# The inverse of the softmax sums on VectorE in place of ScalarE, with a new order of the work

## The chip, the cores and the metric

The kernel runs on one core of a Trainium2 chip. The metric is the device time of one execution in microseconds (us). Every comparison is between runs on the same chip. The profile names the engines PE (TensorE matmuls), PEld (TensorE weight loads), DVE (VectorE), ACT (ScalarE), POOL (GpSimd) and SP (SyncE, which issues most DMAs).

## The reference

The program is a transformer block over 2048 tokens of width 640: layernorm, an attention with a recurrent memory and a residual, then layernorm, a gated feed-forward part (width 1728) and a residual. The attention goes through 64 segments of 32 tokens in sequence. Each segment attends to 8 memory rows and its own 32 tokens, with 32 heads of 128, and the memory of the next segment is the attention's output at the 8 memory rows. So segment s + 1 cannot start its projections of the memory before segment s is through its output projection.

```
mem = mem0
for s in range(n_seg):
    h = jnp.concatenate([mem, xs], axis=1)          # 8 + 32 rows
    q, k, v = h Wq, h Wk, h Wv                      # per head
    scores = where(mask, q k^T * scale, -1e9)
    p = _softmax(scores, axis=-1)
    o = (p v) Wo
    mem = o[:, :M, :]
    outs.append(o[:, M:, :])
```

The softmax divides the exponentials by their sum over the 40 keys. The kernel computes the inverse of each sum and multiplies the exponentials by it. That inverse is what the change is about.

## The kernel before, in words

Weights are loaded once and stay in SBUF. The attention's main part treats 32 rows per segment, the 8 memory rows and the first 24 tokens; the last 8 tokens of the segments do not depend on the memory, and their projections are made ahead, 32 rows at a time for four segments, by `rest` (from L1567), as work that fills gaps of the recurrence. Layernorms (`ln1`, `ln2`), and the output projection of the 8 last tokens (`rest_o`, L1637), are such fill work too. After the 64 segments comes the feed-forward part (`ffn`, L1717).

One segment (`segment`, L1839) does the following, in two groups g of 16 heads:

- `main_qk` and `main_v` project the 32 rows to queries, keys and values (L1561 is the matmul of all projections). The results are evacuated from PSUM to `tok` (Q0ev, K0ev, Q1ev, K1ev) and turned by VectorE's 32x32 transposes into QT and KT (Q0Tev, K0Tev, Q1Tev, K1Tev, L1981), or evacuated to `Vm` (V0ev, V1ev). Evacuations go through the helper at L1399 to L1402: L1401 is the ScalarE form, L1402 the VectorE form.
- `scores(g)` (L1851): the mask is written into a PSUM bank (seed), TensorE adds the scores to it (sc, L1860 and L1864), ScalarE takes the exponentials into E (exp, L1869), and TensorE sums them over the keys by matmuls with a block of ones (sum, L1874 and L1539), into columns 224 to 384 of the same bank, so that each sum stands at the partitions of its keys, 128x160 in fp32.
- The inverse of the sums is made by ScalarE in two instructions: the logarithm of the bank into `lnS` (L1882), then exp(-x) of `lnS` into `rS`, in bf16 (L1884). VectorE multiplies E by rS in place (mul, L1886). There is one lnS and one rS for both groups, so the second group's inverse waits until the first multiplication has read rS.
- `pv(g)` (L1892): TensorE multiplies the scaled exponentials with the values (L1899 and L1904), and two copies bring the result to `oT` (oTev).
- The output projection: group 0 by `wo_early` (L1932), whose result is split into two bf16 halves (hiev, loev at L1940), group 1 by `wo` (L1951), to which the halves are added by matmuls (woadd, L1968; L1539 again). `mem_next` (L1665) copies the memory rows into the next input (L1673) and transposes it to xT (L1676), which the next segment's projections read.

**The order of the work** is set by a list scheduler in the kernel's own code (`_Sched`). Every step is declared with its engine or engines, its reads and writes, and a duration `dur`. Its level is the longest path of declared durations from it to the end, plus two numbers from the table BIAS: one for its name ("rec0": the inverse of group 0) and one for its name in one segment ("rec0@20"). Among steps that can start at nearly the same time on an engine the one with the highest level goes first. Each engine then has one fixed order of instructions, with semaphore waits on the others. For evacuations that ScalarE or VectorE could do, the table ENGINE fixes the engine, by name or by name and segment; those that are not in it go where the declared durations let them end first. BIAS and ENGINE hold numbers found by a search. DMAs are issued in the same way, mostly on SP's queue.

Of the kernel before, what the change touches and what calls it, by code (L numbers as in the profile page):

```python
# [6 lines left out]
F32 = mybir.dt.float32  # L7
# [15 lines left out]
BIAS = {"ldrs": 7992.0, "ldv": 8028.08, "QK0mm": 104.65, "r0Tev": 14.09, "memev": 167.3, "ln2n": 144.44,  # L23
# [12 lines left out]
    "ordma": 158.72, "oTr": 169.2, "rsdma": -179.29, "l1e2": 169.29, "down": -59.94, "ln2Tev": -117.41,  # L36
# [7 lines left out]
    "K0T": 89.89, "QK1mm": 50.37, "free": -27.64, "ervdma": -169.96, "erdma": -49.67, "rvdma": 188.66,  # L44
    "free0": -32.62, "woadd": -36.1, "sel2": 60.17, "loev": -192.29, "hiev": 1.72, "ezero": 80.29,
# [1216 lines left out]
def build_kernel(nc, A_x, A_mem0, A_Wq, A_Wk, A_Wv, A_Wo, A_seg_len, B_x, B_W_gate, B_W_up,  # L1262
# [108 lines left out]
    def bank(b):  # L1371
        return ps[:, b.at * 512:(b.at + 1) * 512]
# [774 lines left out]
```

## Time and profile before

Three runs took 1050.64, 1051.72 and 1053.94 us. The rest of the table is from one profiled execution.

| what | value |
| --- | --- |
| median of the runs | 1051.72 us |
| span of the profiled execution, first to last instruction | 1051.2 us |
| mean granted TensorE clock | 0.995 |
| TensorE busy | 993.4 us, 95% |
| VectorE busy | 652.5 us, 62% |
| ScalarE busy | 488.1 us, 46% |
| logarithm of the sums (L1882, ScalarE) | 128 x 302 ns |
| exponential of its negative (L1884, ScalarE) | 128 x 336 ns |
| multiplication of E by the inverse (L1886, VectorE) | 128 x 334 ns |
| first, middle and last stage of the span | 0 to 75, 75 to 862, 862 to 1051.2 us |

How to read it: in the first stage the weights come in and the first segments run, in the middle stage run nearly all segments, the last stage is the feed-forward part. The profile gives for each group of instructions its busy time, the mean duration of one, and the idle time of the engine just before it with what ended that idle time. Matmuls are pipelined, so that a busy TensorE is not yet one at its peak. A weight load that waits is the first sign that TensorE's queue waits. For the profiled execution there is the span and no other time; it lies 0.5 us under the median of the runs.

### The profile page before, as it was taken

How to read it: one execution, taken by the hardware profiler on the slowest of the kernel's cores; microseconds unless marked ns; L12 is line 12 of the kernel's file. 1: busy time of each engine (PE TensorE's matmuls, PEld its weight loads, DVE VectorE, ACT ScalarE, POOL GpSimd, SP SyncE). 2: the span in 40 equal slices, each digit the busy share in tenths (PEclk: the TensorE clock that was granted, in tenths of full speed). 3: DMA queues.
4: the chain of work that ended last, by engine and by line, in shares of the span. 5: the costliest groups of instructions: out<-in, count | busy, mean ns of one | idle time of the engine just before them, and what ended most of it. 6: DMA issues, size and time to landing. Idle time of an engine off the chain costs nothing.

```text
span 1051.2 us, 53190 instructions
## 1 busy us (share of the span) xinstructions
PE 993.4 (95%) x24820; PEld 534.8 (51%) x23828; DVE 652.5 (62%) x1404; ACT 488.1 (46%) x1161; POOL 108.4 (10%) x262
## 2 busy tenths in 40 slices
PE   5699999999999999999999999999999989999998
PEld 2245555655565555655555555655555444444443
DVE  4457767677777767776777677667865642432233
ACT  2334555455556545555665455645554632121210
POOL 2301101011011101110101011011110010000000
PEclk9999999999999999999999999999999999999999
DMA  9991112121222112221222122212211237111101
GB/s 328 397 286 47 49 37 55 32 54 50 80 54 73 38 42 60 73 66 33 80 69 54 32 69 58 66 28 76 70 49 31 77 117 219 65 38 44 32 20 57
DMA packets 119212, 84.26 MB, mean 80 GB/s; under 512 B 71556, under 2 KB 115148, under 8 KB 118988
## 3 DMA queue, kind: packets, MB, share of 16 engines
q1 hardware_dynamic: 115628, 78.13, 24.9%
q8 instruction: 191, 3.13, 1.3%
q10 hardware_dynamic: 3360, 2.73, 0.8%
q14 instruction: 33, 0.27, 0.1%
HBM read 55.05 MB, written 25.69 MB: 77 GB/s over the span
## 4 chain that ended last, share of the span: by engine, by line
PE 86%; DVE 4%; ACT 2%; issue 2%; DMA 1%; ACTq 0%; POOL 0%; SPq 0%
PE ps L1561 45%; PE ps L1729 11%; PE ps L1932 7%; PE ps L1951 7%; PE ps L1762 5%; PE ps L1647 3%; PE ps L1899 2%; PE ps L1539 2%; PE ps L1874 1%; PE ps L1860 1%; DVE xT L1676 1%; DVE xm L1673 1%; DVE oT L1402 1%; DMA RS<-stg 1%; ACTq L1605 0%
## 5 line engine op out<-in xcount | busy, mean ns | idle before, releaser
L1401 ACT ACTIVATE tok<-ps 128x512 bf16<-128x512 f32 x241 | 142.2, 596 | 177.6 <-PE ps L1561 162.5
L1561 PE MATMUL ps<-Wk,xT 128*32 128x512 bf16 x2560 | 178.0, 380 | 14.2 <-DVE xT L1676 10.2
L1561 PE MATMUL ps<-Wq,xT 128*32 128x512 bf16 x2560 | 178.4, 379 | 6.1 <-DVE xT L1676 6.0
L1561 PE MATMUL ps<-Wv,xT 128*32 128x512 bf16 x2560 | 175.2, 380 | 0.2 <-DMA Wv<-in_A_Wv_dram 0.2
L1981 DVE STREAM_TRANSPOSE KT<-tok 128x512 bf16<-128x512 bf16 x128 | 89.6, 704 | 35.2 <-ACT tok L1401 33.7
L1981 DVE STREAM_TRANSPOSE QT<-tok 128x512 bf16<-128x512 bf16 x128 | 90.3, 706 | 32.8 <-ACT tok L1401 30.1
L1561 PEld LDWEIGHTS ps<-Wk,xT 128*32 128x32 bf16 x2560 | 67.1, 96 | 82.3 <-DVE xT L1676 20.9
L1561 PEld LDWEIGHTS ps<-Wq,xT 128*32 128x32 bf16 x2560 | 67.5, 96 | 72.2 <-DVE xT L1676 12.2
L1402 DVE CAST oT<-ps 128x320 bf16<-128x320 f32 x127 | 60.3, 488 | 54.7 <-PE ps L1904 51.8
L1932 PE MATMUL ps<-Wo,oT 128*32 128x320 bf16 x2048 | 90.9, 300 | 3.3 <-DVE oT L1402 3.2
L1951 PE MATMUL ps<-Wo,oT 128*32 128x160 bf16 x4096 | 86.2, 233 | 6.6 <-issue 4.9
L1746 ACT ACTIVATE g<-ps 128x512 bf16<-128x512 f32 (+1 forms) x56 | 33.4, 596 | 124.8 <-PE ps L1729 124.8
L1951 PEld LDWEIGHTS ps<-Wo,oT 128*32 128x32 bf16 x4096 | 74.3, 97 | 22.2 <-DVE oT L1402 9.5
L1748 DVE TENSOR_TENSOR gT<-g,ps 128x512 bf16<-128x512 bf16 (+1 forms) x56 | 37.5, 686 | 77.3 <-PE ps L1729 47.1
L1401 ACT ACTIVATE oT<-ps 128x320 bf16<-128x320 f32 x129 | 54.0, 435 | 54.9 <-PE ps L1904 53.2
L1561 PEld LDWEIGHTS ps<-Wv,xT 128*32 128x32 bf16 x2560 | 59.7, 96 | 38.0 <-ACT tok L1401 1.0
L1846 POOL COPY QT<-RS 128x256 bf16<-128x256 bf16 x64 | 25.8, 403 | 457.6 <-PE ps L1864 457.1
L1402 DVE CAST tok<-ps 128x512 bf16<-128x512 f32 x79 | 52.9, 670 | 24.8 <-PE ps L1561 24.5
L1869 ACT ACTIVATE E<-ps 128x224 bf16<-128x224 f32 x128 | 45.6, 356 | 43.0 <-PE ps L1864 42.2
L1729 PE MATMUL ps<-xn2T,Wg 128*128 128x512 bf16 x260 | 63.3, 379 | 0.3 <-DVE gT L1748 0.3
L1729 PE MATMUL ps<-xn2T,Wu 128*128 128x512 bf16 x260 | 63.3, 379 | 0.0
L1762 PE MATMUL ps<-Wd,gT 128*128 128x512 bf16 x224 | 61.7, 379 | 0.0
(93 smaller groups left out, 1444.6 us busy)
## 6 DMA issues: line engine op xcount, KB each, us to landing
RS<-scr_qk SPq DMA_DIRECT2D x63, 128.0 KB, 2.3
big<-in_A_x_dram SPq DMA_DIRECT2D x36, 160.0 KB, 2.8
scr_qk<-stg SPq DMA_DIRECT2D x44, 128.0 KB, 2.2
Wq<-in_A_Wq_dram SPq DMA_DIRECT2D x10, 512.0 KB, 7.3
Wk<-in_A_Wk_dram SPq DMA_DIRECT2D x10, 512.0 KB, 7.4
Wv<-in_A_Wv_dram SPq DMA_DIRECT2D x10, 512.0 KB, 8.1
Wo<-in_A_Wo_dram SPq DMA_DIRECT2D x8, 640.0 KB, 10.8
scr_v<-stg SPq DMA_DIRECT2D x32, 128.0 KB, 2.7
```

The costliest lines, as they stand in the source:

```text
L1401: return e.activation(dst, src, ACTF.Copy)
L1402: return e.tensor_copy(dst, src)
L1561: o = pe.matmul(out, lhs[c], rhs, start=(c == 0), stop=(c == DC - 1), skip_group_check=True)
L1647: o = pe.matmul(bank(bk)[p0:p0 + 32, 0:2 * SLICE], oTr[b][:, 16 * g + 4 * j + i, 32 * y:32 * y + 32], cols(h, 2 * a, 2 * a + 2), start=(h ...
L1729: o = pe.matmul(bank(bk)[:, 0:TB], lhs(c), xT[:, :, c * 128:(c + 1) * 128], start=(c == 0), stop=(c == DC - 1))
L1746: op("act", lambda a, t=t, lo=lo, hi=hi, bg=bg: a.activation(g1[t.at][lo:128, :], bank(bg)[0:hi, 0:TB], ACTF.Relu), r=["B2"], x=[bg, t], d ...
L1748: op("dve", lambda v, t=t, lo=lo, j=j, bu=bu: v.tensor_tensor(gT[lo:128, j, :], g1[t.at][lo:128, :], bank(bu)[lo:128, 0:TB], ALU.mult), r= ...
L1762: pe.matmul(bank(ba)[:, 0:512], lhs, Wd[:, j, 0:512], start=(j == 0), stop=(j == FC - 1), skip_group_check=True)
L1869: op("act", lambda a: a.activation(E[:, g, :, 0:56], sco(BS[g]), ACTF.Exp, scale=SCALE), r=["table"], w=[("E", g)], x=[BS[g]], dur=0.36, n ...
L1932: o = pe.matmul(bank(BA)[p0:p0 + 32, 0:2 * SLICE], oT[:, 4 * jj + i, XR:40], cols(h, 2 * b2, 2 * b2 + 2), start=(i == 0 and jj < 2), stop= ...
L1951: o = pe.matmul(bank(BW)[32 * j:32 * j + 32, 0:SLICE], oT[:, 16 + 4 * jj + i, XR:40], cols(h, j, j + 1), start=(i == 0 and jj == 0), stop= ...
L1981: op("dve", lambda v, tb=tb, dst=dst: v.transpose(dst, tok[tb.at][:, :].rearrange("p (h r) -> p h r", r=32)), w=[("QT" if p == 0 else "KT" ...
```

## The change

The inverse of the sums is one VectorE instruction, a reciprocal that reads the sums in PSUM and writes rS in bf16. The logarithm and the exponential of ScalarE go away, and with them the tile lnS. The step keeps its name (rec0, rec1) and its declared duration of 0.33. Nothing else of the computation changes.

All numbers of BIAS and ENGINE are others: BIAS goes from 3499 entries to 3410 with none of them equal, ENGINE from 689 to 442. So the order of the instructions on every engine, and the engine of many evacuations, change too. Of those that the tables fix on VectorE over the 64 segments: V0ev from 23 to 3, V1ev from 44 to 1, K0ev from 24 to 1, K1ev from 5 to 3, Q0ev from 8 to 10, Q1ev from 33 to 48. Before, 30 of Q0ev and 24 of K1ev were left to the declared durations; after, none of these six names.

```
-BIAS = {"ldrs": 7992.0, "ldv": 8028.08, "QK0mm": 104.65, "r0Tev": 14.09, "memev": 167.3, "ln2n": 144.44,
...
-    "er1T": 151.28, "er0T": 20.42, "ln1T": 213.1, "sum1": 44.27, "rec0": -93.01, "ln2nd": 109.66,
...
-    "mul0": 111.45, "mask0": 49.23, "Q1Tev": 309.11, "ln0": 40.86, "mask1": 16.89, "V1mm": -24.65,
...
+    "Q1ev": 317.41, "Q1Tev": 643.59, "K1ev": -113.73, "K1Tev": -250.28, "V1mm": -33.96, "V1ev": -82.6,
+    "seed0": -24.36, "sc0": -20.28, "exp0": -610.44, "sum0": 35.39, "rec0": -70.29, "mul0": 375.41,
...
-    "K0ev": "dve", "er0ev": "act", "r1ev": "dve", "rvev": "act", "Q0Tev": "act", "osbev": "act",
...
+ENGINE = {"er0Tev": "act", "er1ev": "act", "Q0ev": "act", "Q0Tev": "act", "K0ev": "act", "K0Tev": "act",
+    "V0ev": "act", "Q1ev": "dve", "Q1Tev": "dve", "K1ev": "act", "K1Tev": "act", "V1ev": "act", "seed1": "act",
...
@@ -1323,7 +1270,6 @@
     E = ar.alloc("E", [128, 2, 4, 80], BF16)
-    lnS = ar.alloc("lnS", [128, 160], F32)
     rS = ar.alloc("rS", [128, 160], BF16)
...
@@ -1879,10 +1825,10 @@
-            op("act", lambda a: a.activation(lnS[:, :], bank(BS[g])[:, 224:384], ACTF.Ln),
-               r=["table"], w=["lnS"], x=[BS[g]], dur=0.3, name=f"ln{g}")
-            op("act", lambda a: a.activation(rS[:, :], lnS[:, :], ACTF.Exp, scale=-1.0),
-               r=["lnS"], w=["rS"], dur=0.33, name=f"rec{g}")
+            def inverse(v):
+                with nc.allow_low_precision(reason="the sums' inverses are of the inputs' type"):
+                    return v.reciprocal(rS[:, :], bank(BS[g])[:, 224:384])
+            op("dve", inverse, w=["rS"], x=[BS[g]], dur=0.33, name=f"rec{g}")
```

More of the change, by code (lines that the diff above doesn't have):

```diff
@@ L22 @@
 ADD = 4
-BIAS = {"ldrs": 7992.0, "ldv": 8028.08, "QK0mm": 104.65, "r0Tev": 14.09, "memev": 167.3, "ln2n": 144.44,
[12 rows of a table removed]
-    "ordma": 158.72, "oTr": 169.2, "rsdma": -179.29, "l1e2": 169.29, "down": -59.94, "ln2Tev": -117.41,
[7 rows of a table removed]
-    "K0T": 89.89, "QK1mm": 50.37, "free": -27.64, "ervdma": -169.96, "erdma": -49.67, "rvdma": 188.66,
-    "free0": -32.62, "woadd": -36.1, "sel2": 60.17, "loev": -192.29, "hiev": 1.72, "ezero": 80.29,
[586 rows of a table removed]
-ENGINE = {"Q1Tev": "dve", "r0Tev": "act", "V1ev": "dve", "l1e0": "dve", "l1e2": "dve", "ln2Tev": "act",
-    "K0ev": "dve", "er0ev": "act", "r1ev": "dve", "rvev": "act", "Q0Tev": "act", "osbev": "act",
[131 rows of a table removed]
+BIAS = {"sel2": -441.65, "ezero": 172.26, "ldxrs0": 410.57, "ldxrs1": 812.23, "ldxra": -143.87, "ldxrl": 370.82,
+    "ldxrx": -190.47, "ldxrn": -453.78, "ln1rT": -359.59, "l1r": -21.49, "ldxs0": 455.91, "ldxs1": -311.66,
+    "ldxa": 459.65, "ldxl": 162.16, "ldxx": -63.35, "ldxn": 474.64, "ldxx0": -54.04, "ldxst": 103.86,
+    "ldxxm": -394.13, "ldmev": 106.07, "ones": 26.56, "mem": 217.62, "mem1": 70.53, "er0mm": -202.35,
[19 rows of a table added]
+    "tn2nd": 179.14, "gu": -56.84, "relu": 128.7, "gmul": -267.28, "hld": 284.67, "down": -60.53,
[583 rows of a table added]
+ENGINE = {"er0Tev": "act", "er1ev": "act", "Q0ev": "act", "Q0Tev": "act", "K0ev": "act", "K0Tev": "act",
+    "V0ev": "act", "Q1ev": "dve", "Q1Tev": "dve", "K1ev": "act", "K1Tev": "act", "V1ev": "act", "seed1": "act",
+    "r0ev": "act", "r0Tev": "act", "r1ev": "act", "osrev": "act", "ln2Tev": "act", "tn2Tev": "act",
[79 rows of a table added]
 class _Slot:
```

1413 rows, old and new, of tables (BIAS, ENGINE) are left out of this document.

## The prediction

> **What bounds the kernel.** I read the page from the top, then the busy time by stage, then the waits of TensorE's weight loads in the middle stage, and last one segment on VectorE and ScalarE in order of time.
>
> ```profile
> span 1051.2 us, 53190 instructions
> ...
> PE 993.4 (95%) x24820; PEld 534.8 (51%) x23828; DVE 652.5 (62%) x1404; ACT 488.1 (46%) x1161; POOL 108.4 (10%) x262
> ...
> PE 86%; DVE 4%; ACT 2%; issue 2%; DMA 1%; ACTq 0%; POOL 0%; SPq 0%
> ```
> TensorE is busy for 95% of the span and makes up 86% of the chain that ended last; ScalarE, which the change relieves, is 2% of that chain.
>
> ```profile
> core 0: us, PE busy (x) PEld busy (x) DVE busy (x) ACT busy (x) POOL busy (x), PEclk, DMA share, GB/s
> 0.00:75.00 75.00, 52.59 (x988) 22.51 (x980) 34.95 (x80) 21.90 (x46) 18.80 (x47) 0.95 0.98 344
> 75.00:862.00 787.00, 755.76 (x22662) 433.56 (x21902) 560.32 (x1226) 430.15 (x1052) 89.60 (x215) 1.00 0.22 58
> ```
> The middle stage holds nearly all segments. TensorE is idle there for 787.0 - 755.8 = 31.2 us. VectorE is busy for 71%, ScalarE for 55%: the inverse goes from the less busy of the two to the busier one.
>
> ```profile
> PEld ps L1561 <- DVE xT L1676: 32.3, 54, 1.1
> PEld ps L1874 <- ACT E L1869: 26.5, 84, 0.7
> PEld ps L1899 <- DVE E L1886: 20.5, 67, 0.8
> ```
> These are weight loads of the middle stage. The third line is what the inverse can delay: the load of the value product (L1899) waits for the scaled E of L1886 in 67 of 128 groups, 0.31 us each. TensorE itself often still works off earlier matmuls then, so not all of the 20.5 us is lost. I counted the chain that ended last piece by piece: the logarithm (L1882) is on it 10 times with 2.9 us, the exponential (L1884) 10 times with 3.4 us. In the other 118 groups the pair is beside TensorE's work.
>
> **The rows of the change.**
>
> ```profile
> L1882 ACT ACTIVATE lnS<-ps 128x160 f32<-128x160 f32 x128 | 38.7, 302 | 23.7 <-PE ps L1539 23.4
> L1884 ACT ACTIVATE rS<-lnS 128x160 bf16<-128x160 f32 x128 | 43.0, 336 | 4.2 <-DVE E L1886 0.3
> L1886 DVE TENSOR_TENSOR E<-E,rS 128x320 bf16<-128x320 bf16 x128 | 42.8, 334 | 14.8 <-ACT rS L1884 12.2
> L1402 DVE CAST Vm<-ps 128x512 bf16<-128x512 f32 x67 | 45.3, 675 | 4.4 <-PE ps L1561 4.1
> L1402 DVE CAST osb<-ps 128x160 bf16<-128x160 f32 x20 | 5.7, 287 | 9.0 <-PE ps L1539 9.0
> ```
> Removed: 128 x (302 + 336) ns = 81.7 us of ScalarE, of which 6.3 us are on the chain. VectorE's multiplication waited for this pair in only 19 groups (12.2 us, by the waits on rS); in the other 109 VectorE was still busy with something else when the inverse was ready.
>
> Added: 128 reciprocals on VectorE, 128x160, fp32 in PSUM to bf16 in SBUF. No row shows one. The lower bound is the copy of the same shape, between the same memories, on the same engine: 287 ns. The upper bound I build from the slope of the two copy rows, (675 - 287) / (512 - 160) = 1.10 ns per column, so one pass over 160 columns is 0.18 us and 0.11 us is fixed. A quotient has to be developed to the 8 significant bits of the bf16 result; at one pass per bit, that is 0.11 + 8 x 0.18 = 1.5 us, an estimate. For the low end speaks ScalarE, where the logarithm of 160 columns (302 ns) costs what a copy of 160 does. For the high end speaks that every VectorE row of this trace adds, multiplies, compares or moves, so that the copy is near in shape and not in kind, and that the only inverse of the page takes two whole instructions on its engine. I take the upper end, with little lead, and keep both for the range.
>
> [...]
>
> Moved: the tables fix 67 evacuations of V on VectorE in the old order and 4 in the new one. 63 x 675 ns = 42.5 us leave VectorE, and about 63 x 0.59 = 37 us come to ScalarE (its row for V, 591 ns). With the copy's price the reciprocals add 128 x 0.287 = 36.7 us, and VectorE stays where it was; with 1.5 us they add 192 us, and its load in the middle stage is 560 + 189 - 42 = 707 of 787 us, 90%. ScalarE ends lower either way (430 - 80 + 37) and costs nothing. Dropping lnS moves no work. No DMA is added; loads and stores change places only as the new order has it, and the middle stage uses 22% of the DMA engines.
>
> The added wait: the reciprocal waits on VectorE for TensorE's sums. Behind it stand the multiplication, the second query transpose, which the second scores wait for, and the copies of oT, which the output projection waits for. One segment shows what it meets:
>
> ```profile
> 451.81 0.65 DVE L1402 CAST tok<-ps 128x512 bf16<-128x512 f32 x1
> 452.50 0.71 DVE L1981 STREAM_TRANSPOSE QT<-tok 128x512 bf16<-128x512 bf16 x1
> 453.14 0.28 DVE L1886 TENSOR_TENSOR E<-E,rS 128x320 bf16<-128x320 bf16 x1
> 454.23 0.49 DVE L1402 CAST oT<-ps 128x320 bf16<-128x320 f32 x1 [0.81 <-PE ps L1904]
> 454.75 0.69 DVE L1402 CAST Vm<-ps 128x512 bf16<-128x512 f32 x1
> 455.35 0.32 DVE L1886 TENSOR_TENSOR E<-E,rS 128x320 bf16<-128x320 bf16 x1
> 456.25 0.49 DVE L1402 CAST oT<-ps 128x320 bf16<-128x320 f32 x1 [0.59 <-PE ps L1904]
> ```
> Here the first logarithm began at 452.09, while VectorE ran the copy and the transpose of the second queries until 453.21. Put behind that transpose (the new table gives Q1Tev a far higher bias than rec0), a reciprocal of 1.5 us ends at 454.7, the multiplication at 455.0, and the first value product starts 1.2 us late. The second reciprocal runs from 455.0, the second multiplication ends near 456.9 where it ended at 455.67: again 1.2 us. That is one delay, carried along. Put ahead of the transpose, it delays the second scores by 1.5 us and the second value product by about 2.2 us. TensorE's order is fixed, and from the second value product on the segment has no work to spare: output projection, new memory (L1673), its transpose (L1676), next segment. The plan itself is laid for a short reciprocal (the code declares 0.33), so it does not cover the rest.
>
> **The sum.** 63 segments in the stage after the first, times 1.2 us, is 75.6 us. Its own bounds: 0.7 us where VectorE's idle time and fill work on TensorE take part of it (44 us), 1.8 us where the reciprocal often stands ahead of the transpose (113 us). 1051.2 + 75.6 = 1126.8. The median of the runs, 1051.72, is 0.5 us above the profiled span, so I add 0.5: **about 1127 us**, with 1096 to 1165 for this case.
>
> **The rivals.** A difference under 0.3% (3.2 us) is about what a measurement of this kernel cannot tell from none.
>
> Second: the reciprocal costs what the copy costs, and the pair was hidden anyway. The chain gains 6.3 us and pays ten reciprocals, 2.9 us; the new order gives and takes as much. That is 1049 to 1055, say 1051. For it speaks that the pair is on the chain in 10 of 128 groups; against it, that the whole order is another one.
>
> Third, on the other side: at the copy's price the change is faster. The inverse is one instruction of 0.29 us with one handover less, in place of 0.64; the chain gains 6.3 - 2.9 = 3.4 us, and the order, with V's evacuations off VectorE ahead of the transposes, wins back a sixth of TensorE's 31.2 us of idle time, 5.2 us: 1051.7 - 8.6 = 1043, down to 1035 at twice that. It decides from the point where VectorE is free when the sums land. Against it: it was free in 19 of 128 groups.
>
> Fourth: the copy's price, but VectorE is not free. In the 67 groups where the weight load waited for E, 0.287 us is added, 19.2 us, less the 6.3 us that leave the chain: 1051.7 + 12.9 = 1065, and 1055 to 1075.
>
> **How the numbers follow.** Forecast 0.52, second 0.14, third 0.24, fourth 0.10. Slower is first and fourth, 0.62; same 0.14; faster 0.24. The range reaches from 1040, which leaves out about 0.1 of the third rival, to 1165, which leaves out under 0.1 of the forecast; both prices of the reciprocal are in it.
>
> **What would show it.** The reciprocal's row: over 1 us for the forecast, about 0.29 us for the rivals; between them the sum shrinks in proportion. With the forecast, VectorE's busy time in the middle stage rises by over 100 us, the weight loads of L1899 wait for E in nearly all groups and for far more than 20.5 us, and the time comes in the middle stage alone, with the last stage still near 189 us. The forecast is wrong if the row is long and the middle stage is not: then VectorE's idle time (227 us of 787) covered it. If the row is short, second to fourth are told apart by the waits on E and by how often VectorE is busy when the sums land.

## The result and the profile after

The changed kernel takes 1108.96 us, the median of four runs (1106.79 to 1111.61), against 1052.83 us before. The ratio is 1.0538, with a 95% interval from 1.0506 to 1.0570. The profiled execution of the changed kernel has a span of 1109.8 us, 58.6 us more than before.

The page of the changed kernel, its head, busy times and the chain that ended last:

```profile
span 1109.8 us, 53145 instructions
...
PE 995.1 (90%) x24808; PEld 538.0 (48%) x23828; DVE 740.7 (67%) x1432; ACT 465.6 (42%) x1005; POOL 108.2 (10%) x262
...
PE 64%; DVE 24%; ACT 3%; issue 2%; ACTq 1%; DMA 0%; POOL 0%; DVEq 0%
PE ps L1507 30%; DVE rS L1830 13%; PE ps L1675 11%; PE ps L1897 7%; PE ps L1878 4%; PE ps L1708 4%; DVE KT L1927 3%; DVE E L1832 3%; ACT tok L1347 3%; PE ps L1845 3%; DVE oT L1348 2%; PE ps L1485 2%; PE ps L1593 2%; DVE stat L1421 1%; DVE QT L1927 1%
```
TensorE has nearly the same work, 995.1 us after 993.4, now 90% of the span. On the chain VectorE goes from 4% to 24%, and one line of it, the reciprocal (L1830), has 13%. Counted piece by piece, the reciprocal is on the chain 127 times out of 128, with 141 us. The ScalarE pair before was on it 10 times, with 6.3 us.

The rows of the step by form, changed kernel (busy us, mean ns of one, idle time ahead of it and what ended that):

```profile
L1830 DVE RECIPROCAL rS<-ps 128x160 bf16<-128x160 f32 x128 | 147.5, 1152 | 13.0 <-PE ps L1485 12.8
L1832 DVE TENSOR_TENSOR E<-E,rS 128x320 bf16<-128x320 bf16 x128 | 41.5, 324 | 4.1
L1348 DVE CAST Vm<-ps 128x512 bf16<-128x512 f32 x4 | 2.7, 680 | 0.0
```
One reciprocal takes 1.152 us, 3.6 times what the copy of the same shape takes (0.320 us in e1 below). The V evacuations left VectorE as the tables say. And VectorE was idle until the sums came in only 24 of 128 groups; otherwise it was busy when they landed.

The middle stage of the changed kernel, with the columns of before, and who waits there (in the last three fences first the wait of TensorE's matmuls before the change, then the waits of the matmuls and of the weight loads after it; us in all, times, longest):

```profile
75.00:920.00 845.00, 760.07 (x22654) 436.31 (x21891) 647.89 (x1262) 407.91 (x896) 88.36 (x214) 0.99 0.20 53
```
```profile
PE ps L1899 <- DVE E L1886: 0.5, 2, 0.3
```
```profile
PE ps L1845 <- DVE E L1832: 60.3, 98, 1.6
PE ps L1507 <- DVE xT L1622: 5.2, 12, 0.6
```
```profile
PEld ps L1845 <- DVE E L1832: 101.2, 98, 1.8
```
The stage is 58.0 us longer (845.0 against 787.0), nearly all of the 58.6 us, and TensorE is idle in it for 845.0 - 760.1 = 84.9 us, where it was 31.2. The ends of the stage were set by hand, but the feed-forward's own start says the same: its first matmul is at 928.0 us in place of 868.7. The value product's weight loads (L1845; in the kernel before, L1899) wait for the scaled E in 98 groups for 101.2 us, where it was 67 groups and 20.5 us; and now TensorE itself stands still there, 60.3 us, where it was 0.5.

One segment on the chain that ended last (start us, us, what):

```profile
472.35 0.71 DVE KT L1927
473.06 1.12 DVE rS L1830
474.18 0.02 issue
474.20 0.34 DVE E L1832
474.54 0.05 issue
474.58 0.27 PE ps L1845 x16
474.86 0.09 PE ps L1850 x4
474.94 0.02 issue
474.97 0.49 DVE oT L1348
475.46 1.07 DVE rS L1830
476.53 0.03 issue
476.56 0.33 DVE E L1832
476.89 0.05 issue
476.94 0.27 PE ps L1845 x16
```
Every link is VectorE or the value product that waits for it. The first reciprocal begins when VectorE is through a key transpose, the sums having landed just before. The second begins behind the copy of the first product's result (L1348), so it cannot start before the first reciprocal, the first multiplication and the first product are through. In the same segment TensorE stands idle for 0.62 us ahead of the first value product and for 0.64 us ahead of the second. Its rows (the number in brackets is the idle time and what ended it) show a second reason why the second reciprocal is late:

```profile
474.58 0.27 PE L1845 MATMUL ps<-E,Vm 32*128 32x40 bf16 x16 [0.62 <-DVE E L1832]
...
474.82 0.25 PE L1820 MATMUL ps<-E,bones 128*32 128x160 bf16 x4
...
476.94 0.27 PE L1845 MATMUL ps<-E,Vm 32*128 32x40 bf16 x16 [0.64 <-DVE E L1832]
```
TensorE makes the sums of the second group (L1820) only after the first value product, so they too are late when that product is. In this order that is so in 57 of the 64 segments, and in 39 a copy of the first product's result is the VectorE instruction just ahead of the second reciprocal.

### The profile page after: what moved, and what is told of

Same layout as the page of the kernel before. It is cut to its first block, busy times and chain, and to the rows that moved or that the text cites. A ratio compares the mean times of both kernels' runs of the same rounds, so it can differ in the third digit from the quotient of the medians.

```text
span 1109.8 us, 53145 instructions
## 1 busy us (share of the span) xinstructions
PE 995.1 (90%) x24808; PEld 538.0 (48%) x23828; DVE 740.7 (67%) x1432; ACT 465.6 (42%) x1005; POOL 108.2 (10%) x262
## 4 chain that ended last, share of the span: by engine, by line
PE 64%; DVE 24%; ACT 3%; issue 2%; ACTq 1%; DMA 0%; POOL 0%; DVEq 0%
PE ps L1507 30%; DVE rS L1830 13%; PE ps L1675 11%; PE ps L1897 7%; PE ps L1878 4%; PE ps L1708 4%; DVE KT L1927 3%; DVE E L1832 3%; ACT tok L1347 3%; PE ps L1845 3%; DVE oT L1348 2%; PE ps L1485 2%; PE ps L1593 2%; DVE stat L1421 1%; DVE QT L1927 1%
## 5 line engine op out<-in xcount | busy, mean ns | idle before, releaser
L1347 ACT ACTIVATE tok<-ps 128x512 bf16<-128x512 f32 x248 | 147.2, 597 | 220.3 <-PE ps L1507 207.9
L1507 PE MATMUL ps<-Wq,xT 128*32 128x512 bf16 x2560 | 170.6, 379 | 5.4 <-DVE xT L1622 5.2
L1507 PE MATMUL ps<-Wk,xT 128*32 128x512 bf16 x2560 | 171.1, 379 | 4.3 <-DMA Wk<-in_A_Wk_dram 4.2
L1830 DVE RECIPROCAL rS<-ps 128x160 bf16<-128x160 f32 x128 | 147.5, 1152 | 13.0 <-PE ps L1485 12.8
L1347 ACT ACTIVATE oT<-ps 128x320 bf16<-128x320 f32 x144 | 60.8, 436 | 127.9 <-PE ps L1850 126.1
L1507 PEld LDWEIGHTS ps<-Wq,xT 128*32 128x32 bf16 x2560 | 67.2, 96 | 74.6 <-DVE xT L1622 18.3
L1845 PE MATMUL ps<-E,Vm 32*128 32x40 bf16 x2048 | 35.2, 178 | 70.8 <-DVE E L1832 60.7
L1347 ACT ACTIVATE Vm<-ps 128x512 bf16<-128x512 f32 x124 | 74.0, 597 | 29.5 <-PE ps L1507 29.4
L1845 PEld LDWEIGHTS ps<-E,Vm 32*128 32x128 bf16 x2048 | 22.1, 91 | 122.2 <-DVE E L1832 102.0
L1348 DVE CAST oT<-ps 128x320 bf16<-128x320 f32 x112 | 54.1, 487 | 33.0 <-PE ps L1850 32.3
L1347 ACT ACTIVATE ps<-seed 128x384 f32<-128x384 bf16 x109 | 50.2, 487 | 49.6 <-DVE half L1886 42.0
```

Source lines behind the costliest of these rows:

```text
L1347: return e.activation(dst, src, ACTF.Copy)
L1348: return e.tensor_copy(dst, src)
L1507: o = pe.matmul(out, lhs[c], rhs, start=(c == 0), stop=(c == DC - 1), skip_group_check=True)
L1830: return v.reciprocal(rS[:, :], bank(BS[g])[:, 224:384])
L1845: o = pe.matmul(bank(BP[j])[:, 40 * i:40 * i + 40], Vm[32 * j:32 * j + 32, g, i * 128:(i + 1) * 128], E[32 * j:32 * j + 32, g, i, 0:40], s ...
```

## The experiments

Theory A: the length of the reciprocal is the whole loss. The rivals: B, it is the move to VectorE's busy queue or the new order, whatever the instruction costs; C, it is that the plan was laid for 0.33 us and did not know the length. Theories D and E, on how the two groups' delays add up, come with e7 and e8. "New tables" and "the order of the change" are the change's BIAS and ENGINE, "old tables" those of before. The scheduler lays the order from tables and declared durations, so a kernel that keeps both keeps the order, whatever the instruction in the step really is. The runs were made on several chips, each with the kernel before beside it, so times of different runs are compared by their ratios to it; a ratio is turned into us with 1052 us.

### e1: a copy in the place of the reciprocal

```
-                    return v.reciprocal(rS[:, :], bank(BS[g])[:, 224:384])
+                    return v.tensor_copy(rS[:, :], bank(BS[g])[:, 224:384])
```


> The changed kernel with the reciprocal replaced by a copy of the same 128x160 from PSUM to rS, on the same engine, at the same place of the same order; the multiplication then uses the sums themselves, so the scaling is not the reference's. Theory A (the 1152 ns of the reciprocal are the whole loss): the row falls to about 0.29 us, the waits of the value product's weight loads for E fall from 101 us to under 30 us, and the time is 1042 to 1056 us. Rival B (the loss is the move of the inverse to VectorE's queue, or the new order, whatever the instruction takes): 1080 us or more.

1041.81 us; ratio to the kernel before 0.9913 (0.9886 to 0.9940). The step's row, and the waits for E of the value product's weight loads and matmuls:

```profile
L1830 DVE CAST rS<-ps 128x160 bf16<-128x160 f32 x128 | 40.9, 320 | 12.5 <-PE ps L1485 12.0
```
```profile
PEld ps L1845 <- DVE E L1832: 34.8, 92, 1.0
...
PE ps L1845 <- DVE E L1832: 0.8, 1, 0.8
```
Same engine, same place, same order, 0.83 us less in each group: 67 us less (66 by the ratios), just under the range expected, and faster than the kernel before by 0.9%. So the move to VectorE and the new order, taken together, are no loss at the length of a copy; B falls. The weight loads still wait 34.8 us, a little over the 30 expected, but TensorE's own wait for E falls from 60.7 us to 0.8 us: at this length the waiting is covered by matmuls under way.

### e2: the ScalarE pair back, with the new tables

```
-            op("dve", inverse, w=["rS"], x=[BS[g]], dur=0.33, name=f"rec{g}")
+            op("act", lambda a: a.activation(lnS[:, :], bank(BS[g])[:, 224:384], ACTF.Ln), ...
+            op("act", lambda a: a.activation(rS[:, :], lnS[:, :], ACTF.Exp, scale=-1.0), ...
```


> The changed kernel with its new tables, and the logarithm and exponential of ScalarE put back in place of the reciprocal. Theory A: the tables alone cost little, 1045 to 1065 us. Rival B (the new order is what is slow): 1080 us or more.

1092.88 us, ratio 1.0394 (1.0374 to 1.0414). By its expectation this is B, but e1 ran the order of the change at 0.9913, so that order is not slow. e2 does not run it: with other steps the same tables lay another plan (in order of time at most 574 of the change's 1432 VectorE instructions keep their order). That the pair is slow here because the tables were found for another step fits this, and is not shown apart. VectorE now waits for rS (last column: idle ahead of the multiplication):

```profile
L1833 DVE TENSOR_TENSOR E<-E,rS 128x320 bf16<-128x320 bf16 x128 | 41.6, 325 | 64.2 <-ACT rS L1831 63.7
```
64 us of waiting for ScalarE, where it was 12.2 us in all before. Taken alone, this run would have misled.

### e3: only the reciprocal, with the old tables

The kernel before with the hunk on the inverse alone, BIAS and ENGINE as they were.

> The kernel before with its old tables, and only the inverse changed to the reciprocal. Theory A: as slow as the change or slower, since VectorE keeps the evacuations of V too: 1108 to 1135 us. Rival B (the new order is what is slow): clearly faster than the change, under 1090 us.

1159.72 us, ratio 1.1019 (1.0999 to 1.1038): slower than expected, and 50 us slower than the change. The new tables do not make the change slow, they save about half of what this hunk alone costs (10.2% against 5.4%).

### e4: the real length declared, with the new tables

```
-            op("dve", inverse, w=["rS"], x=[BS[g]], dur=0.33, name=f"rec{g}")
+            op("dve", inverse, w=["rS"], x=[BS[g]], dur=1.15, name=f"rec{g}")
```


> The changed kernel with the same tables, and the reciprocal declared to the scheduler at 1.15 in place of 0.33, so that the order is laid for its real length. Theory A (the length is on the recurrence and cannot be filled): 1095 to 1115 us. Rival C (the loss is that the plan did not know the length, and TensorE has fill work to put there): under 1085 us.

1119.71 us, ratio 1.0643 (1.0618 to 1.0667): 11 us slower than the change, above what was expected. Declaring the length is no help without tables found for it. The plan is a different one (at most 671 of 1432 VectorE instructions keep their order): TensorE's wait for E falls from 60.7 to 18.3 us, and its wait for the next segment's input rises from 5.2 to 29.0.

```profile
PE ps L1507 <- DVE xT L1622: 29.0, 56, 1.0
PE ps L1845 <- DVE E L1832: 18.3, 28, 1.6
```
These waits do not explain the 11 us. Over the whole span TensorE is idle for 1118.1 - 1006.6 = 111.5 us, where the change has 1109.8 - 995.1 = 114.7. What is longer is its busy time, by 11.5 us, at a granted clock of 0.985 against 0.993; why, no run shows.

### e5: a copy with the old tables

The kernel of e3 with the copy of e1.

> The kernel before with its old tables, the inverse replaced by a copy on VectorE (so the scaling is not the reference's). With e3 it gives the price of the reciprocal's length in another order; with the kernel before, the price of tables that were searched for another step. Theory A with the length priced as in the new order (1109 - 1042 = 67 us): 1160 - 67 = 1093, so 1080 to 1105 us. Rival B' (in the old tables the reciprocal costs little by its length, and the move to VectorE costs most): 1125 us or more.

1079.79 us, ratio 1.0256 (1.0217 to 1.0296), a hair under the lower edge of what was expected. In the old tables too the length of the reciprocal is what costs: from e5 to e3 (1.0256 to 1.1019) it is 7.6%, 80 us, where it is 66 us in the new ones. (Of the 77.7 us between the two profiled spans, TensorE's idle time makes up 66.7 and its busy time 11.0.) The other 2.6% are what the move to VectorE costs in tables that were found for the pair; no run parts the move from the tables.

### e6: a touch on the plan

The kernel before, the same instructions, the logarithm declared at 0.31 in place of 0.30.

> The kernel before, same instructions and same tables; only the declared duration of the logarithm goes from 0.30 to 0.31, so that the order is laid again without a search. If the tables fit one set of declared durations and no other, the time rises to 1070 to 1100 us, and e2, e3 and e4 each carry such a surcharge. If they are robust: 1050 to 1058 us, and e2's 1093 is a loss of the new order itself.

1055.49 us, ratio 1.0042 (1.0020 to 1.0063). That lies in the range for robust tables, but it tests little, because the plan hardly changed: in order of time up to 1397 of VectorE's 1404 instructions and 1156 of ScalarE's 1161 stand as before. What a plan laid anew costs, as in e2 and e4, this run does not tell, so the surcharges of e2, e4 and e5 stay mixtures of the step and its plan.

### e7 and e8: the reciprocal in one group only

```
-                    return v.reciprocal(rS[:, :], bank(BS[g])[:, 224:384])
+                    f = v.reciprocal if g == 0 else v.tensor_copy      # e8: g == 1
+                    return f(rS[:, :], bank(BS[g])[:, 224:384])
```


> The order of the change, reciprocal in group 0, copy in group 1 (so group 1's scaling is not the reference's). Theory D (the prediction: one delay is carried along, and the second inverse decides): 1042 to 1060 us. Theory E (two separate stalls of TensorE at the two value products, 0.6 us each by the trace): half of the 67 us, 1068 to 1085 us.

> The order of the change, copy in group 0 (so group 0's scaling is not the reference's), reciprocal in group 1. Theory D: nearly all of the 67 us, 1092 to 1110 us. Theory E: about half, 1068 to 1085 us, and the two surcharges of e7 and e8 add up to that of the change.

e7: 1076.63 us, ratio 1.0230 (1.0193 to 1.0268). e8: 1066.65 us, ratio 1.0139 (1.0103 to 1.0175), a little under its range for theory E. Above the copy in both groups (0.9913) these are 3.2% and 2.3%, 33 us and 24 us; together 57 us, where both reciprocals cost 6.25%, 66 us. The waits of TensorE for E, first of e7, then of e8:

```profile
PE ps L1846 <- DVE E L1833: 33.7, 52, 1.6
```
```profile
PE ps L1846 <- DVE E L1833: 27.4, 47, 0.8
```
33.7 us of standing still for 33 us of time, 27.4 us for 24 us. In the traces, e7's wait lies in group 0 alone, e8's in group 1 but for 0.8 us, and the change itself has 33.6 us in group 0 and 27.0 in group 1. There are two stalls in a segment, and they add up to 57 of the 66 us; the other 9 us come only with both reciprocals, and no run says from where. Theory D, one delay that is carried along and decided by the second inverse, falls.

### e9 and e10: other lengths of the step

e9 makes the reciprocal twice, the first time into a scratch tile. e10 makes 80 columns by a copy and 80 by a reciprocal.

```
+                    v.reciprocal(twice[:, :], bank(BS[g])[:, 224:384])                      # e9
                     return v.reciprocal(rS[:, :], bank(BS[g])[:, 224:384])
```
```
+                    v.tensor_copy(rS[:, 0:80], bank(BS[g])[:, 224:304])                     # e10
+                    return v.reciprocal(rS[:, 80:160], bank(BS[g])[:, 304:384])
```


> The order of the change, with the reciprocal made twice in the same step (the first time into a scratch tile), so the step takes about 2.3 us. From the copy (0.29 us) to the reciprocal (1.15 us) the time rose by 67 us for 0.86 us more, 0.61 us per us and group over 128 groups. Theory A, with all cover used up: from here each further us comes in full, 128 x 1.15 = 147 us more, 1245 to 1265 us. Rival (the slope of 0.61 goes on, since part of the work stays beside it): 1190 to 1210 us.

> The order of the change; 80 of the 160 columns by a copy and 80 by a reciprocal, two instructions (so half of the scaling is not the reference's). By length the step is about 0.2 + 0.63 = 0.83 us. If each us beyond the cover comes in full, the cover is 0.86 - 67 / 128 = 0.34 us beyond the copy, and 0.83 - 0.29 - 0.34 = 0.20 us x 128 = 26 us remain: 1062 to 1075 us. By an even slope of 0.61: 1042 + 0.54 x 0.61 x 128 = 1084 us.

e9: 1246.09 us, ratio 1.1829 (1.1783 to 1.1875). e10: 1074.36 us, ratio 1.0211 (1.0183 to 1.0239). With the lengths from their own rows (e10: 236 + 648 ns; e9: 1153 + 1095 ns), and the time as ratio times 1052 us:

| step on VectorE, us | time, us | more time per added us and group |
| --- | --- | --- |
| 0.320 (e1, copy) | 1042.8 | |
| 0.884 (e10, half and half) | 1074.2 | 31.4 / (128 x 0.564) = 0.43 |
| 1.152 (the change) | 1108.6 | 34.4 / (128 x 0.268) = 1.0 |
| 2.248 (e9, twice) | 1244.4 | 135.8 / (128 x 1.096) = 0.97 |

From 0.88 us up every microsecond of the step comes in full, or nearly, 128 times. Below that part is covered: if the full price held all the way down, the 31.4 us would be 0.245 us in each group, and so a step of up to 0.320 + 0.564 - 0.245 = 0.64 us would cost nothing in this order. That is an estimate; no run has a step between 0.32 and 0.88 us. Theory A holds in both, and an even slope is ruled out by e9 (1190 to 1210 expected of it) and by e10 (1084).

### e11: the instruction by itself

Reciprocals and copies in a row behind the last output.

> The change with a row of reciprocals and copies behind the last output, to price the instruction by itself: 40, 80, 160 and 320 columns from PSUM, 160 columns from SBUF in fp32 and in bf16, and 160 columns on 32 partitions. If the reciprocal works element by element: 0.11 us and 6.5 ns per column, so about 0.37, 0.63, 1.15 and 2.2 us, the same from SBUF and in bf16, and the same on 32 partitions. If its cost is a fixed start instead: near 1.15 us at all sizes. The time of the whole says nothing here.

VectorE in order of time, at the end of that kernel (start us, us, line, shape), without the copies of 40 and 80 columns:

```profile
1108.52 0.41 DVE L2041 RECIPROCAL tok<-ps 128x40 bf16<-128x40 f32 x1
...
1109.19 0.66 DVE L2041 RECIPROCAL tok<-ps 128x80 bf16<-128x80 f32 x1
...
1110.16 1.16 DVE L2041 RECIPROCAL tok<-ps 128x160 bf16<-128x160 f32 x1
1111.35 0.32 DVE L2042 CAST tok<-ps 128x160 bf16<-128x160 f32 x1
1111.71 2.16 DVE L2041 RECIPROCAL tok<-ps 128x320 bf16<-128x320 f32 x1
1113.90 0.49 DVE L2042 CAST tok<-ps 128x320 bf16<-128x320 f32 x1
1114.42 1.15 DVE L2043 RECIPROCAL tok<-tok 128x160 bf16<-128x160 f32 x1
1115.61 1.15 DVE L2044 RECIPROCAL tok<-tok 128x160 bf16<-128x160 bf16 x1
1116.80 1.15 DVE L2045 RECIPROCAL tok<-ps 32x160 bf16<-32x160 f32 x1
```
By the rows by form the four reciprocals from PSUM take 407, 657, 1157 and 2157 ns: 157 ns and 6.25 ns per column, exactly even, where the copies (324 and 491 ns) grow by 1.04 ns per column. So the cost goes element by element, as the first case expected. Whether the source is PSUM or SBUF, fp32 or bf16, or whether 32 or 128 partitions work, makes next to no difference at 160 columns: 1146 to 1157 ns.

### e12: the tables searched for the real length

> The changed kernel with the reciprocal declared at 1.15, as in e4, and the tables searched further for that length (a short search, 594 evacuations and some 2,800 numbers changed). Theory A (a step of 1.15 us on VectorE stays on the recurrence, whatever the order): above the kernel before, 1070 to 1100 us. Rival C (the whole loss is that the plan did not know the length): 1058 us or less.

1078.28 us, ratio 1.0261 (1.0240 to 1.0282). Against the tables of the change 2808 numbers of BIAS and 477 entries of ENGINE differ, and the order of the weight loads, fixed before, has 46 searched numbers too. With the length known and the tables searched for it, about half of the loss is won back: TensorE waits 13.2 us for E.

```profile
PE ps L821 <- DVE xT L936: 22.5, 46, 0.7
PE ps L1159 <- DVE E L1146: 13.2, 26, 1.6
```
The time is where theory A put it, yet C may have its share: of the change's 5.4%, 2.8% went when the plan knew the length and was searched further. The length alone did not win them (e4); whether a further search at 0.33 would have won some of them was not run. The rest, 2.6%, this order did not remove; whether a longer search would, stays open. No run that scales by the inverse is faster than the kernel before.

## Why the prediction was right, and where not

**The bound.** TensorE makes up the chain before (86%), the inverse lies beside it (6.3 us on the chain), and the inverse moves from the less busy engine (ScalarE, 55% of the middle stage) to the busier one (VectorE, 71%): as the profile said. The loss is in the middle stage (58.0 of 58.6 us), as forecast.

**The price.** I bounded the reciprocal between 0.287 and 1.5 us and took the upper end. It is 1.152 us (e11: 157 ns and 6.25 ns per column). The side was right, the size 30% too high. The reason I gave, one pass per bit of the result, was my estimate and is not shown: the price per column is six times that of the copy (6.25 against 1.04 ns in e11), and no run changed the type of the result.

**The delay per segment.** This step failed in its form. I counted one delay of 1.2 us per segment, carried along, because I let the second reciprocal start directly behind the first multiplication. With the measured 1.152 us the same reckoning gives: first reciprocal 453.21 to 454.36, multiplication to 454.68, where the first value product began at 453.84, so 0.84 us late; second reciprocal to 455.84, multiplication to 456.16, against 455.67 before, so 0.49 us late. Taken as one delay that is 31 us over 63 segments if the second inverse decides, and 53 us if TensorE cannot win back what it lost at the first product. But the second reciprocal cannot start there. The rows of the kernel before, for the same segment, already say so:

```profile
453.84 0.27 PE L1899 MATMUL ps<-E,Vm 32*128 32x40 bf16 x16
...
454.19 0.25 PE L1874 MATMUL ps<-E,bones 128*32 128x160 bf16 x4
```
TensorE makes the second sums after the first value product, so a late product makes them late, and on VectorE the copy of the product stands ahead as well. Each reciprocal therefore makes a stall of its own, and the two add: 33 us and 24 us in e7 and e8, about 0.5 and 0.4 us per segment. That the forecast came near is in part luck: the price was too high and the second stall was missing, and 1.2 us per segment forecast stands against 66 us / 64 = 1.03 us measured against the copy.

**The order.** I gave the new order nothing in the forecast. At the copy's price the new order and the move together gain 0.9%, 9 us (e1), so the change is -9 + 66 = 57 us; the forecast was 76. The third rival's 1043 us is what e1 gives: with a reciprocal as cheap as a copy, that rival's time would have come true, against the second and the fourth. Its two parts, 3.4 and 5.2 us, were not measured apart.

**VectorE's load.** I expected 560 + 147 us in the middle stage; it rose to 648, by 88 us and not by over 100. The reciprocals are 147.5 us in place of 192, and the order moved more than V: the seeds on VectorE fell from 44 to 19, for instance.

**The signs.** The weight loads of L1845 wait for 101 us as foreseen, though in 98 groups and not in nearly all. That the plan "does not cover the rest" is right for the change; e12 shows that a plan laid and searched for the length wins back about half.

## What to carry to other kernels

An instruction that no row of the trace shows is to be priced before an order is laid on it; a row of it behind the last output costs one run and would have settled this change. One instruction in place of two was no gain here: it went to the engine whose queue the critical engine waits for, and took 1.152 us there, where the two took 302 + 336 ns on ScalarE. And an order found by search may lose much of its worth with another step in it (e2, e4 and e5 point that way): to learn what an instruction costs, change what the step executes and keep the plan (e1, e9), not the plan with it (e2, e4).

## What the runs showed of the hardware that was not expected

VectorE's reciprocal costs 157 ns and 6.25 ns per column from 40 to 320 columns: 1.157 us for 160 columns, where a copy takes 0.324 us, and within 1% of that for an SBUF or a bf16 source or 32 partitions (e11). ScalarE's pair of logarithm and exponential on the same 160 columns, 302 + 336 ns, is the faster inverse by a factor of 1.8 in this kernel.
